# Moving four blocks of a bias table into its main run and three others behind the first scores

## The chip, the cores and the metric

One Trainium2 chip, one of its cores. The time is the device time of one execution in microseconds; for the kernel before it is the median of three runs.

## The reference

Attention with a learned relative bias, then a mixture of experts. Shapes: 8 batches, 8 heads, 576 positions, head size 64, hidden size 32 for the bias.

```python
scores = scale * q @ k.T
psi_rel = log1p(abs(i - j)); psi_i = log1p(max(i, 1))
h = relu((psi_rel / psi_i) * w1 + b1)        # 32 hidden per (i, j)
scores += h @ w2                              # 576 x 576, one per head
attn = softmax(scores); out = attn @ v
# then every token goes through its best of 8 experts, times its gate
```

The bias does not depend on the batch. It is made once, as a table in SBUF, and added to every batch's scores.

## The kernel before

**The table.** The query rows are made in 36 blocks (NBLK). A block covers 16 query rows for all 8 heads: four column groups (cg), each with one hidden tile of 128 partitions (4 rows x 32 hidden) by 576 keys, `relu(window of tg + shift)`, made by `bias_hidden` on ScalarE (L189) for cg 0 and on VectorE (L191) for the others; two matmuls for each (`bias_out`, L199) into PSUM; and one put (`bias_put`): a scaled copy from PSUM on ScalarE (L215) or, for the blocks in PUT_DVE, on VectorE (L213), into one of eight output buffers taken in turn (bias_outs), and from there by DMA into the table. Blocks 0 to 31 (NMAIN) fill `NBm`, the first 512 query rows: block `8c + k` writes rows k, k + 8, ... of the heads of query chunk c, with one DMA (L218) of 288 KB. Blocks 32 to 35 fill `NBr`, the last 64 query rows of two heads at a time, with four DMAs (L223) of 72 KB each. All of these DMAs go through SP's queue, in program order, as do the loads of q, k and v.

**The main run** (`bias_table`) goes through blocks 0 to 31 with three PSUM tiles of two banks. ScalarE's hidden is made one block ahead, and a put is issued one block later (LAG). Hooks run at given blocks: loads and transposes of q and k, steps of the routing's set-up. The table's last blocks are generators (`bias_late`): the first step makes the four hidden, the second the matmuls, into a bank of `eps` and one of `xps`, and the put.

**Attention** (`attention`) goes through pairs of heads n, in five units u each; unit u of a pair makes the scores of 128 queries of both heads (units 0 to 3) or of the last 64 queries of both (unit 4). `ORDER` gives each unit's steps by letters; S is `scores`: twelve matmuls (six in unit 4) into `sps` (L400), and on VectorE the reduction L414 for each head, which adds the table (NBm for units 0 to 3, NBr for unit 4), stores the sum and its minimum. e and f are the exponentials (L429 on ScalarE), t and T the transposes (L444, two units behind), q and k VectorE's transposes of the next pair's q and k. The engines run their instructions in the order written. Unit 3 needs blocks 24 to 31, unit 4 blocks 32 to 35.

In the kernel before the main run ends with the four hidden of block 32, and `LATE` gives the steps of blocks 32 to 35 at the head of units 0 and 1 of the first pair, ahead of their scores; `load_v(0)` follows them at unit 1 (V0). The part of `attention` that places them:

```python
for u, k in self.LATE:
    tail.setdefault((0, u), []).append(lambda k=k: next(self.late[k], None))
tail.setdefault(self.V0, []).append(lambda: self.load_v(0))
```

PSUM: the three tiles of the main run lie where `attn_late` then puts sps0, sps1 and the two eps banks, so the first scores wait for the puts of the last main blocks that used those tiles. SBUF: hidden tiles lie in `eT`, `rT` and, in the main run only, in `Eb`.

Of the kernel before, what the change touches and what calls it, by code (L numbers as in the profile page):

```python
# [40 lines left out]
NMAIN = P // 4  # L41
NBLK = S4 // 4
# [9 lines left out]
def bias_base(blk, cg):  # L52

    if blk < NMAIN:
        return P * (blk // GS) + blk % GS + 4 * GS * cg
    return 4 * P + 2 * (blk - NMAIN) + cg // 2 + 4 * GS * (cg % 2)
# [52 lines left out]
class Attn:  # L109
# [8 lines left out]

    ON_POOL, ON_DVE = (), (1,)


    LAG = 1
    PUT_DVE, ON_ACT2 = (21, 31, 34), ()
    TURN0, SPLIT0, QK1 = (4, 8), (6, 10), (9, 10, 11, 12, 13, 14, 15, 16)
    V0 = (0, 1)
    ROUTE = (6, 7, 8, 15, 16, 18)

    ROUTE_LATE = ((1, 1), (1, 2), (1, 3), (1, 4), (2, 0), (2, 1), (2, 3), (3, 0), (3, 1))  # L130

    LATE_HIDDEN = ((31, 0),)
    LATE = ((0, 1), (0, 0), (0, 2), (0, 1), (0, 3), (1, 2), (1, 3))

    def bias_setup(self):

# [43 lines left out]
    def bias_hidden(self, blk, cg, by):  # L180

        nc = self.nc
        s = bias_base(blk, cg)
        win = self.tg[:, X0 - s : X0 - s + S]
        c = self.shift[:, 4 * blk + cg : 4 * blk + cg + 1]
        h = next(h for h in self.bias_free if blk < NMAIN or not any(h is x for x in self.bias_main))
        self.bias_free = [x for x in self.bias_free if x is not h]
        if by == "act":
            nc.scalar.activation(h, win, AF.Relu, bias=c)  # L189
        else:  # L190
            (nc.gpsimd if by == "pool" else nc.vector).tensor_scalar(h, win, c, 0.0, op0=ALU.add, op1=ALU.max)  # L191
        return h
# [32 lines left out]
    def bias_table(self, hooks):  # L225

        ready = {}
        self.late = [self.bias_late(blk) for blk in range(NMAIN, NBLK)]

        def ahead(blk, cg):  # L230
            if blk < NMAIN and (blk, cg) not in ready:
                by = "pool" if cg == 3 and blk in self.ON_POOL else "act" if cg == 0 and blk not in self.ON_DVE or cg == 1 and blk in self.ON_ACT2 else "dve"
                ready[blk, cg] = self.bias_hidden(blk, cg, by)

        with self.tc.tile_pool(name="bps", bufs=3, space=PSUM) as pp:
            done = []
            for blk in range(NMAIN):
                ps = pp.tile([P, 1024], F32, tag="bps", name=f"bps{blk}")
                if blk + 3 in self.ON_POOL:
                    ahead(blk + 3, 3)  # L240
                for k in range(2):
                    if blk + k not in self.ON_DVE:
                        ahead(blk + k, 0)
                    if blk + k in self.ON_ACT2:
                        ahead(blk + k, 1)
                for cg in range(4):
                    ahead(blk, cg)
                    self.bias_out(cg, ready.pop((blk, cg)), (ps[:, 0:512], ps[:, 512:S]))
                for at, k in self.LATE_HIDDEN:
                    if at == blk:  # L250
                        next(self.late[k])
                if len(done) == self.LAG:
                    self.bias_put(*done.pop(0))
                done.append((blk, [(slice(0, S), ps[:, 0:S])]))
                for f in hooks.get(blk, ()):
                    f()
            for d in done:
                self.bias_put(*d)
# [299 lines left out]
    def attention(self):  # L558
        n_pair = self.n_pair
        tail = self.first_tiles() if self.K else {}  # L560
        for at in self.ROUTE_LATE:
            tail.setdefault(at, []).append(lambda: next(self.route, None))
        for u, k in self.LATE:
            tail.setdefault((0, u), []).append(lambda k=k: next(self.late[k], None))
        tail.setdefault(self.V0, []).append(lambda: self.load_v(0))
        bg = None
        for n in range(n_pair + 1):
            for u in range(5):
                for f in tail.get((n, u), ()):
                    f()  # L570
                if n == 1 and u == 0:
                    bg = self.blanks()
                if u == 4 and n > 0 and n % NP == 0:
                    assert not bg or all(k == len(x) for x, k in bg)
                    bg = self.route_steps(n // NP - 1)
                m, w = (n, u - 2) if u >= 2 else (n - 1, u + 3)
                scored = []
                for op in self.ORDER[u].split():
                    op, self.defer = op[0], int(op[1:] or 0)
                    if op in "aAbc":  # L580
                        self.flush(lambda x: x[0][0] in "er")
                    elif op == "X":
                        self.flush(lambda x: x[0][0] == "a")
                    self.held = [] if self.defer and op in "tTRAc" else None
                    if op in "SefC":
                        if n == n_pair:
                            continue
                        if op == "S":
                            scored = self.scores(n, u)
                        elif op == "C":  # L590
                            self.compact(n, u)
                        else:
                            self.exps(*scored["ef".index(op)])
                    elif op in "tT":
                        if 0 <= m < n_pair:
                            self.etrans(m, w, "tT".index(op))
                    elif op == "x":
                        if n > 0:
                            self.flush(lambda x: x[0][:2] == "av")
                            self.turn_x(n - 1)  # L600
                    elif op in "RaAbc":
                        if n > 0:
                            self.rtrans(n - 1) if op == "R" else self.av(n - 1, *divmod("aAbc".index(op), 2))
                    elif op in "qk01V":
                        if n + 1 < n_pair:
                            if op == "V":
                                self.load_v(n + 1)
                            elif op in "qk":
                                self.turn(n + 1, "qk".index(op))
                            else:  # L610
                                self.split(n + 1, int(op))
                    elif op == "L":
                        if n + 2 < n_pair:
                            self.load_qk(n + 2)
                    elif f := self.route_next(bg, "XB".index(op)):
                        f()
                    fresh, self.held = self.held or [], None
                    for x in self.waiting:
                        x[2] -= 1
                    self.flush(lambda x: x[2] <= 0)  # L620
                    self.waiting += fresh
                if 0 <= m < n_pair:
                    del self.E[m, w]
        self.flush(lambda x: True)
        self.bg = bg
# [867 lines left out]
```

## Time and profile before

| | |
|---|---|
| median of three runs | 1006.18 us (1005.96 to 1006.64) |
| the profiled execution's own time | 1007.5 us |
| its span | 1005.4 us |
| TensorE busy | 972.1 us, 97% |
| VectorE, ScalarE busy | 709.4 us, 712.7 us |
| GpSimd busy | 303.1 us |
| mean granted TensorE clock | 0.995 |

The span is what lies between the first and the last recorded instruction; the execution's own time has what is around it too. In rows, PE is TensorE, PEld its weight loads, DVE VectorE, ACT ScalarE, POOL GpSimd, SP the engine that issues the DMAs; SPq, DVEq and so on are the sequencers. A row of a timeline has a start, a length, the engine, the line in the kernel, the operation, what it writes and reads, its shape, how many are merged, and in brackets how long the engine had been idle and what ended that. A granted clock of 1.00 is TensorE's upper level, 2.4 GHz, and 0.50 its lower, 1.2 GHz.

### The profile page before, as it was taken

How to read it: one execution, taken by the hardware profiler on the slowest of the kernel's cores; microseconds unless marked ns; L12 is line 12 of the kernel's file. 1: busy time of each engine (PE TensorE's matmuls, PEld its weight loads, DVE VectorE, ACT ScalarE, POOL GpSimd, SP SyncE). 2: the span in 40 equal slices, each digit the busy share in tenths (PEclk: the TensorE clock that was granted, in tenths of full speed). 3: DMA queues.
4: the chain of work that ended last, by engine and by line, in shares of the span. 5: the costliest groups of instructions: out<-in, count | busy, mean ns of one | idle time of the engine just before them, and what ended most of it. 6: DMA issues, size and time to landing. Idle time of an engine off the chain costs nothing. (4 is left out here: it accounts for less than half of the span.)

```text
span 1005.4 us, 22478 instructions
## 1 busy us (share of the span) xinstructions
PE 972.1 (97%) x8110; PEld 762.4 (76%) x8110; DVE 709.4 (71%) x1441; ACT 712.7 (71%) x1366; POOL 303.1 (30%) x489
## 2 busy tenths in 40 slices
PE   7969999999999999999999899999999999999997
PEld 4547767767677676776667589889999998989896
DVE  8965768776777777777877677886666656565655
ACT  7977988888888888888888555455555555454554
POOL 1512433625426254262542513511111111111111
PEclk9998999999999999999999999999999999999999
DMA  6977755564655646546469430312117821162610
GB/s 163 194 166 152 196 104 116 109 131 101 128 108 105 134 100 120 119 101 133 94 121 212 128 112 32 96 48 64 43 43 190 271 64 54 61 195 68 186 43 24
DMA packets 327417, 116.34 MB, mean 116 GB/s; under 512 B 283247, under 2 KB 304111, under 8 KB 327299
## 3 DMA queue, kind: packets, MB, share of 16 engines
q1 hardware_dynamic: 321234, 95.80, 43.3%
q0 software_dynamic: 5920, 19.03, 5.4%
q8 instruction: 65, 1.06, 0.5%
q14 instruction: 54, 0.43, 0.2%
q10 hardware_dynamic: 144, 0.00, 0.0%
HBM read 144.34 MB, written 33.34 MB: 177 GB/s over the span
## 5 line engine op out<-in xcount | busy, mean ns | idle before, releaser
L414 DVE CUSTOM_DVE_ANT_0 Eb<-sps,NBm 128x576 f32<-128x576 f32 x256 | 183.6, 754 | 125.0 <-PE sps L400 57.1
L429 ACT ACTIVATE Eb<-Eb,mn 128x576 f32<-128x576 f32 x288 | 221.0, 769 | 13.6 <-DVE mn L414 12.6
L332 ACT ACTIVATE eT<-eps 128x512 f32<-128x512 f32 x256 | 148.9, 595 | 55.7 <-PE eps L444 54.8
L400 PE MATMUL sps<-QK 64*128 64x288 f32 (+1 forms) x1728 | 171.7, 310 | 7.5 <-DVE mn L414 7.0
L400 PEld LDWEIGHTS sps<-QK 64*128 64x128 f32 (+1 forms) x1728 | 134.3, 186 | 48.1 <-DVE mn L414 29.6
L1212 PE MATMUL p<-QK,w1hi 128*128 128x256 f32 x1136 | 161.8, 285 | 2.8 <-DVE QK L1196 2.2
L444 PE MATMUL eps<-idf,Eb 128*128 128x128 f32 x1024 | 149.6, 280 | 3.6 <-DVE eT L334 1.9
L1212 PEld LDWEIGHTS p<-QK,w1hi 128*128 128x128 f32 x1136 | 147.1, 191 | 7.3 <-DVE QK L1196 3.0
L486 PE MATMUL xps<-eT,vraw 128*64 128x288 f32 x1024 | 149.3, 416 | 0.0
L444 PEld LDWEIGHTS eps<-idf,Eb 128*128 128x128 f32 x1024 | 113.3, 141 | 37.5 <-issue 13.6
L1238 POOL DMA_INDIRECT out<-mo,idt x36 | 39.5, 1099 | 308.1 <-ACT mo L1237 252.4
L1214 ACT ACTIVATE hh<-p 128x512 fp32r<-128x512 f32 x72 | 43.1, 598 | 123.0 <-PE p L1212 116.7
L1215 DVE SCALAR_TENSOR_TENSOR hl<-p,hh 128x512 fp32r<-128x512 f32 x72 | 49.7, 691 | 101.6 <-ACT hh L1214 97.8
L1229 PE MATMUL p<-w2hi,hh 128*128 128x512 f32 x288 | 112.3, 390 | 0.0
L1229 PE MATMUL p<-w2hi,hl 128*128 128x512 f32 x288 | 112.3, 390 | 0.0
L434 POOL COPY rem<-Eb 128x128 f32<-128x128 f32 x128 | 37.0, 291 | 244.1 <-ACT Eb L429 238.3
L1174 DVE TENSOR_TENSOR w2lo<-NBm,w2hi 128x1024 fp32r<-128x1024 f32 x72 | 89.5, 1243 | 16.0 <-ACT w2hi L1173 15.7
L486 PEld LDWEIGHTS xps<-eT,vraw 128*64 128x64 f32 x1024 | 62.3, 136 | 39.9 <-issue 12.4
L1212 PE MATMUL p<-QK,w1lo 128*128 128x256 f32 x568 | 91.2, 283 | 0.0
L1174 DVE TENSOR_TENSOR w1lo<-NBm,w1hi 128x1024 fp32r<-128x1024 f32 x72 | 85.0, 1243 | 0.0
L1212 PEld LDWEIGHTS p<-QK,w1lo 128*128 128x128 f32 x568 | 78.3, 192 | 0.0
L1173 ACT CAST w2hi<-NBm 128x1024 fp32r<-128x1024 f32 x72 | 74.9, 1040 | 0.0
(219 smaller groups left out, 1451.0 us busy)
## 6 DMA issues: line engine op xcount, KB each, us to landing
NBm<-moe_w SPq DMA_DIRECT2D x84, 512.0 KB
NBm<-moe_w SPq DMA_DIRECT2D x42, 1024.0 KB
NBr<-xg SPq DMA_DIRECT2D x80, 128.0 KB
kraw<-k SPq DMA_DIRECT2D x128, 72.0 KB
xd<-xt SPq DMA_DIRECT2D x128, 72.0 KB
vraw<-v SPq DMA_DIRECT2D x64, 128.0 KB
NBm<-xTb SPq DMA_DIRECT2D x24, 288.0 KB
NBm<-moe_w SPq DMA_DIRECT2D x3, 2048.0 KB
```

The source lines that it names most:

```text
L332: self.nc.scalar.activation(out, ps, AF.Copy, scale=scale)
L400: nc.tensor.matmul(self.sps[h][:, half, 0:HS], QK[o, q, qs], QK[o, k, HS * half : HS * half + HS], start=i == 0, stop=i == 2, skip_group_c ...
L414: nc.vector.tensor_tensor_reduce(out=e.rearrange("p (t w) -> p t w", t=2), in0=self.sps[h][:, :, 0:HS], in1=nb.rearrange("p (t w) -> p t w ...
L429: self.nc.scalar.activation(e, e, AF.Exp, bias=mn, scale=-1.0, accum_out=sm)
L444: nc.tensor.transpose(ps[:, k, :], e[:, part, P * k : P * k + P], self.idf)
L486: nc.tensor.matmul(ps[out : out + 64, :], lhsT, rhs, tile_position=(row, out), skip_group_check=True, **kw)
L1173: self.nc.scalar.copy(h, w)
L1174: self.nc.vector.tensor_tensor(l, w, h.bitcast(F32), op=ALU.subtract)
L1212: nc.tensor.matmul(ps[:, a, :], w[:, c, fs], x[:, c, :], start=i == 0, stop=i == len(ops) - 1)
L1214: nc.scalar.activation(hh[:, sl, :], ps, AF.Relu)
L1215: nc.vector.scalar_tensor_tensor(hl[:, sl, :], ps, 0.0, hh[:, sl, :].bitcast(F32), op0=ALU.max, op1=ALU.subtract)
L1229: nc.tensor.matmul(ps, h[:, f, sl], m[:, f, :], start=i == 0, stop=i == len(ops) - 1)
```

## The change

The main run now goes by a list, SEQ, of 33 blocks: blocks 0 to 28 in order, with blocks 32, 33, 34 and 35 set in after blocks 7, 11, 15 and 19. Blocks 29, 30 and 31 are made late. Block 29's hidden are made at the end of the main run; its matmuls and put come right behind unit 0's scores, followed by the hidden of blocks 30 and 31; the matmuls and puts of those two come right behind unit 1's scores. Hooks now count positions in SEQ. `load_v(0)` stays at the head of unit 1. PUT_DVE changes from blocks 21, 31, 34 to 21, 29, 31. Two empty options (ON_POOL, ON_ACT2) go.

```diff
--- before.py
+++ after.py
@@ -118,19 +118,19 @@
 
 
 
-    ON_POOL, ON_DVE = (), (1,)
+    ON_DVE = (1,)
 
 
     LAG = 1
-    PUT_DVE, ON_ACT2 = (21, 31, 34), ()
+    PUT_DVE = (21, 29, 31)
     TURN0, SPLIT0, QK1 = (4, 8), (6, 10), (9, 10, 11, 12, 13, 14, 15, 16)
     V0 = (0, 1)
     ROUTE = (6, 7, 8, 15, 16, 18)
 
     ROUTE_LATE = ((1, 1), (1, 2), (1, 3), (1, 4), (2, 0), (2, 1), (2, 3), (3, 0), (3, 1))
 
-    LATE_HIDDEN = ((31, 0),)
-    LATE = ((0, 1), (0, 0), (0, 2), (0, 1), (0, 3), (1, 2), (1, 3))
+    SEQ = (*range(8), 32, *range(8, 12), 33, *range(12, 16), 34, *range(16, 20), 35, *range(20, 29))
+    LATE = ((0, 0), (0, 1), (0, 2), (1, 1), (1, 2))
 
     def bias_setup(self):
 
@@ -183,7 +183,7 @@
         s = bias_base(blk, cg)
         win = self.tg[:, X0 - s : X0 - s + S]
         c = self.shift[:, 4 * blk + cg : 4 * blk + cg + 1]
-        h = next(h for h in self.bias_free if blk < NMAIN or not any(h is x for x in self.bias_main))
+        h = next(h for h in self.bias_free if blk not in self.late_blocks or not any(h is x for x in self.bias_main))
         self.bias_free = [x for x in self.bias_free if x is not h]
         if by == "act":
             nc.scalar.activation(h, win, AF.Relu, bias=c)
@@ -225,34 +225,31 @@
     def bias_table(self, hooks):
 
         ready = {}
-        self.late = [self.bias_late(blk) for blk in range(NMAIN, NBLK)]
+        seq = self.SEQ
+        self.late_blocks = [blk for blk in range(NBLK) if blk not in seq]
+        self.late = [self.bias_late(blk) for blk in self.late_blocks]
 
         def ahead(blk, cg):
-            if blk < NMAIN and (blk, cg) not in ready:
-                by = "pool" if cg == 3 and blk in self.ON_POOL else "act" if cg == 0 and blk not in self.ON_DVE or cg == 1 and blk in self.ON_ACT2 else "dve"
+            if (blk, cg) not in ready:
+                by = "act" if cg == 0 and blk not in self.ON_DVE else "dve"
                 ready[blk, cg] = self.bias_hidden(blk, cg, by)
 
         with self.tc.tile_pool(name="bps", bufs=3, space=PSUM) as pp:
             done = []
-            for blk in range(NMAIN):
+            for at, blk in enumerate(seq):
                 ps = pp.tile([P, 1024], F32, tag="bps", name=f"bps{blk}")
-                if blk + 3 in self.ON_POOL:
-                    ahead(blk + 3, 3)
-                for k in range(2):
-                    if blk + k not in self.ON_DVE:
-                        ahead(blk + k, 0)
-                    if blk + k in self.ON_ACT2:
-                        ahead(blk + k, 1)
+                for b in seq[at : at + 2]:
+                    if b not in self.ON_DVE:
+                        ahead(b, 0)
                 for cg in range(4):
                     ahead(blk, cg)
                     self.bias_out(cg, ready.pop((blk, cg)), (ps[:, 0:512], ps[:, 512:S]))
-                for at, k in self.LATE_HIDDEN:
-                    if at == blk:
-                        next(self.late[k])
+                if at == len(seq) - 1:
+                    next(self.late[0])
                 if len(done) == self.LAG:
                     self.bias_put(*done.pop(0))
                 done.append((blk, [(slice(0, S), ps[:, 0:S])]))
-                for f in hooks.get(blk, ()):
+                for f in hooks.get(at, ()):
                     f()
             for d in done:
                 self.bias_put(*d)
@@ -560,8 +557,6 @@
         tail = self.first_tiles() if self.K else {}
         for at in self.ROUTE_LATE:
             tail.setdefault(at, []).append(lambda: next(self.route, None))
-        for u, k in self.LATE:
-            tail.setdefault((0, u), []).append(lambda k=k: next(self.late[k], None))
         tail.setdefault(self.V0, []).append(lambda: self.load_v(0))
         bg = None
         for n in range(n_pair + 1):
@@ -587,6 +582,8 @@
                             continue
                         if op == "S":
                             scored = self.scores(n, u)
+                            for _, j in (x for x in self.LATE if (n, x[0]) == (0, u)):
+                                next(self.late[j], None)
                         elif op == "C":
                             self.compact(n, u)
                         else:
```

## Rows read from the trace of the kernel before

**Rows 1.** the page, part 1: busy us, share of the span, instructions of each engine

```profile
span 1005.4 us, 22478 instructions
PE 972.1 (97%) x8110; PEld 762.4 (76%) x8110; DVE 709.4 (71%) x1441; ACT 712.7 (71%) x1366; POOL 303.1 (30%) x489
```

**Rows 2.** DVE timeline, 66 to 112 us: start, length, line, operation [idle before <-releaser]

```profile
66.27 0.76 DVE L414 CUSTOM_DVE_ANT_0 Eb<-sps,NBm 128x576 f32<-128x576 f32 x1 [0.44 <-issue]
...
73.68 0.76 DVE L414 CUSTOM_DVE_ANT_0 Eb<-sps,NBr 128x576 f32<-128x576 f32 x1 [4.78 <-DMA vraw<-v]
...
81.34 0.76 DVE L414 CUSTOM_DVE_ANT_0 Eb<-sps,NBm 128x576 f32<-128x576 f32 x1 [3.41 <-PE sps L400]
...
106.26 0.75 DVE L414 CUSTOM_DVE_ANT_0 Eb<-sps,NBr 128x576 f32<-128x576 f32 x1
...
111.22 0.76 DVE L414 CUSTOM_DVE_ANT_0 Eb<-sps,NBm 128x576 f32<-128x576 f32 x1 [1.47 <-PE sps L400]
```

**Rows 3.** timeline of PE (matmuls), 67 to 76 us, same columns

```profile
67.86 1.05 PE L400 MATMUL sps<-QK 128*128 128x288 f32 x6
68.83 1.09 PE L444 MATMUL eps<-idf,Eb 128*128 128x128 f32 x8
74.50 1.81 PE L400 MATMUL sps<-QK 64*128 64x288 f32 x12 [4.58 <-DVE mn L414]
```

**Rows 4.** busy by 2 us stretch: engines, granted clock, DMA share, GB/s

```profile
70.00:72.00 2.00, 0.00 (x0) 0.00 (x0) 0.00 (x0) 0.61 (x2) 0.00 (x0) 1.00 0.40 116
...
74.00:76.00 2.00, 1.50 (x12) 1.46 (x12) 0.45 (x2) 0.87 (x2) 0.00 (x0) 0.50 0.86 143
...
80.00:82.00 2.00, 2.00 (x20) 1.54 (x22) 0.66 (x1) 0.96 (x2) 0.40 (x2) 0.89 0.79 153
```

**Rows 5.** timeline of SP's DMA issues, 44 to 71 us

```profile
44.48 0.55 SPq L218 DMA_DIRECT2D NBm<-xt  x1
...
54.35 0.53 SPq L218 DMA_DIRECT2D NBm<-xt  x1
...
62.83 0.70 SPq L223 DMA_DIRECT2D NBr<-xTb  x1
...
64.14 1.22 SPq L223 DMA_DIRECT2D NBr<-xTb  x2
...
70.59 0.59 SPq L223 DMA_DIRECT2D NBr<-xTb  x1
...
71.22 0.99 SPq L370 DMA_DIRECT2D vraw<-v  x2
```

**Rows 6.** waits of SP's queue, 53 to 80 us: line <- what, us, times, longest

```profile
SPq L223 <- DMA NBm<-xTb: 3.1, 4, 0.9
SPq L223 <- DMA NBm<-xt: 1.0, 2, 0.6
```

**Rows 7.** timeline of DVE, the put of block 31

```profile
53.51 0.82 DVE L213 TENSOR_SCALAR xt<-bps,xrb 128x576 f32<-128x576 f32 x1 [0.58 <-DMA NBm<-xt]
```

**Rows 8.** busy by stretch again: one of 10 us, one of 2 us

```profile
40.00:50.00 10.00, 10.00 (x115) 5.03 (x114) 10.00 (x24) 8.87 (x14) 0.16 (x1) 1.00 1.05 207
...
68.00:70.00 2.00, 1.93 (x15) 1.53 (x14) 0.69 (x1) 2.00 (x6) 1.33 (x2) 1.00 0.38 113
```

**Rows 9.** timeline of DVE: hidden of the last main blocks, then a late put

```profile
50.71 2.22 DVE L191 TENSOR_SCALAR eT<-xTb,xrb 128x576 f32<-128x576 f32 x5
...
59.65 0.74 DVE L213 TENSOR_SCALAR xTb<-eps,xrb 128x512 f32<-128x512 f32 x1
60.31 0.28 DVE L213 TENSOR_SCALAR xTb<-xps,xrb 128x64 f32<-128x64 f32 x1
```

**Rows 10.** timeline of PE: first scores, and the eight matmuls of a late block

```profile
56.85 1.06 PE L400 MATMUL sps<-QK 64*128 64x288 f32 x12
...
57.83 1.09 PE L199 MATMUL eps<-eT,xrb 128*32 128x512 f32 x8
...
59.89 0.22 PE L199 MATMUL xps<-eT,xrb 128*32 128x64 f32 x1
```

## The prediction

> **What bounds the kernel now.** I began with the page: TensorE is busy for 972.1 of 1005.4 us [rows 1], so for nearly the whole span only a place where TensorE waits or runs slowly can give time back. I looked for such places in the stretch that the change touches, the bias table and the first pair (0 to 90 us).
>
> The timeline of VectorE shows one. The first score reduction (L414) of unit 3 of the first pair starts at 66.27. That of unit 4, which alone reads NBr, starts at 73.68 after 4.78 us of idling for a DMA [rows 2]. The row names the load of v, but L414 does not read v; what it reads and what is late is NBr. TensorE has finished everything else by 69.92 (68.83 + 1.09) and idles 4.58 us to 74.50 [rows 3]. It then also runs at half clock: granted 1.00 at 70 to 72 us, 0.50 at 74 to 76, 0.89 at 80 to 82 [rows 4], that is 1.2 GHz until about 80.4 (0.11 of 2 us is 0.44 us at half). What that costs is read from two pairs: from L414 of unit 4 to L414 of the next pair's unit 1 takes 81.34 - 73.68 = 7.66 us there and 111.22 - 106.26 = 4.96 us a pair later [rows 2], so 2.70 us. Stall and clock together are worth about 7.5 us.
>
> Why NBr is late is in SP's issues. Main block 31 was issued at 54.35, but the sixteen NBr DMAs of the four late blocks ran on to 70.59, 0.645 us apart at the end (64.14 to 70.59 is ten steps), and v only follows at 71.22 [rows 5]. Before 64.14 SP's NBr issues waited six times, 4.1 us in all, for older NBm DMAs to land [rows 6]. These waits fit one rule: a DMA is issued when the one eight before it has landed. So block 31's DMA, the eighth before the one at 64.14, took 9.8 us to land. A second sign is the put of block 31, which waits at 53.51 for its buffer, that is for the DMA of block 23 [rows 7], issued at 44.48 [rows 5]: 9.0 us. **The DMA queue is a full eight blocks deep at the end of the table**, one landing each (64.1 - 53.5)/8 = 1.33 us. VectorE is equally full, 10.00 of 10 us, the DMA engines at a share of 1.05 and 207 GB/s; at 68 to 70 us, when only NBr DMAs are out, the share is 0.38 [rows 8].
>
> **Part 1: four blocks of NBr into the main run, three main blocks out.** The work per block is unchanged (four hidden, eight matmuls, one put), and so is the number of blocks. The main run has 33 blocks in place of 32. VectorE pays three hidden for each, five in 2.22 us [rows 9], so 0.44 each and 1.33 a block. In the kernel before, block 32's hidden were already made there, so 33 blocks' hidden end at the same time; block 29's add 1.33, while the put of block 31 on VectorE (0.82 and 0.58 of waiting, [rows 7]) leaves. The first scores need the put of the last block but one, free at about 54.3 (53.5, when its buffer's old DMA has landed, and 0.8), and twelve matmuls of 1.06 us [rows 10]: L414 of unit 0 starts near 55.5.
>
> SP issues four DMAs where it issued one: 3 x 0.645 = 1.9 us more per NBr block, 7.7 us over the run, behind which the later puts queue. It costs TensorE nothing while the eight output buffers cover the delay, and by 47 us, after the last such group, SP is back to one 0.55 us issue per 1.33 us block. If that cover fails, the puts, then PSUM, then TensorE wait.
>
> **Part 2: what is left behind the scores.** VectorE, after unit 0's two reductions (1.4), waits for block 29's matmuls (2.1 from first to last, [rows 10]), puts it (0.74 + 0.28, less overlap 0.95, [rows 9]) and makes six hidden (2.7). Unit 1's L414 then starts near 61.3 (55.5 + 1.4 + about 0.8 of waiting + 0.95 + 2.7); with block 31's put (0.95, ends near 63.7) ahead of the q transpose, unit 3's could start near 67.0, 0.7 later than 66.27. The matmuls of the three blocks lie in TensorE's idle time of this stretch. So the gain of the earlier first scores is spent by unit 3; this is a shift of work between waits, no saving. Behind the put of block 29, which waits for its matmuls on VectorE, stand six hidden and unit 1's reductions; ScalarE's exponentials wait for those.
>
> **Part 3: which wait is last.** NBr lands long before unit 4. But blocks 29 to 31 are rows of NBm that unit 3 reads, one unit sooner, and they are the last in a full queue. SP's order puts the three loads of v, now ahead of unit 1's scores, before blocks 30 and 31. Counting eight back from block 31 (30, three of v, 29, two small ones, the last main block) it cannot be issued before that main block lands, 64.1 + 1.33 = 65.4. Behind it the queue holds block 29, v (as many bytes as a block, costed like one), 30 and 31: 65.4 + 4 x 1.33 = **70.8**. The upper price of an NBr block is a main block's. The lower comes from its own row: share 0.38 x 0.645 = 0.24 us of DMA time per DMA [rows 5, 8], 0.98 per block at a full queue's 1.05 gives 0.93, against 1.33: 0.4 less for each of four, so **69.2**. I take this, the nearest row. At that pace SP's issuing was the limit, the DMA engines were free for most of the time. The Trainium skill, "SBUF — State Buffer", section on the DMA port swizzle, speaks against it: DMA bandwidth depends on how many of SBUF's 16 ports the partitions reach, and by my reading of its map an NBr DMA writes 8 partitions on 4 ports, an NBm DMA 16 on 8. By that page an NBr byte would take twice as long, and the sum would be that of rival 3. The least possible is put (63.7) plus what the last NBr DMA took, 70.59 to 73.68 [rows 2, 5], 3.1: 66.8, which is no wait at all.
>
> From unit 3's L414 to the end of the matmuls ahead of the next pair's first scores there are 69.92 - 66.27 = 3.65 us [rows 2, 3]. The wait stands at the head of VectorE's queue: unit 3's exponentials on ScalarE and unit 4's scores on TensorE wait with it. So the next pair's scores start at 69.2 + 3.65 = 72.85 in place of 74.50: 1.65 gained. TensorE's gap moves forward by a unit: the work ahead of unit 4's scores ends by 67.9 as before, and these start at 69.2 + (67.86 - 66.27) = 70.8 [rows 2, 3]: 2.9 us in place of 4.58. I take it that the clock stays at its upper level then, which gives the 2.70 back. **Sum: -4.35 us.** The profiled execution, to whose rows this belongs, took 1007.5 us around its span of 1005.4; it would take 1003.1. The median of the three runs is 1006.18, which becomes **1001.8 us**. Everything after is bound by TensorE and moves up by the same amount.
>
> **Rivals.**
> 1. Block 31 lands in time (by 67.0). Scores at 70.65: 3.85 + 2.70 = 6.55 gained, **999.6 us**. For it: nothing but the bounds above; against it: queue depth at 54 us.
> 2. The wait only changes its place. The block lands at 70.8, scores start at 74.45, and the gap before unit 4's scores is 4.5 us (72.4 - 67.9), close to the 4.58 after which the clock fell, so it falls again: **1006 us**; with the clock kept, 1003.5. For it: every term of the 70.8 is a measured interval.
> 3. Slower: the NBr DMAs go no faster among the others than alone, 4 x 0.645 = 2.58 us a block against 1.33. Four blocks hold the queue 5.0 us longer, block 31 lands at 75.8, the scores start at 79.45, 4.95 later, with the low clock: **1011 us**. It decides once block 31 lands after 70.9. Against it: at that pace the DMA engines were only 0.38 busy [rows 8], so SP's issuing may have set it. This is the way of the Trainium skill's page "SBUF — State Buffer" above.
> 4. It does not do what it says: unit 4's wait really is for v's queue place [rows 2] or another of SP's, and stays: **1006 us**.
>
> **How the numbers follow.** Forecast 0.38, rival 1 0.20, rival 2 0.22, rival 3 0.10, rival 4 0.10. A measurement of this kernel tells about 0.2% (2 us) from no change. Faster by more than that are the forecast, rival 1 and a little of rival 2 with the clock kept: 0.62; the same: the rest of rival 2, rival 4: 0.28; slower: 0.10. The range leaves out rival 3 and a sliver below rival 1: 999.0 to 1006.6.
>
> **What would show it.** Right: no idle on VectorE before the L414 that reads NBr; a DMA wait of 2 to 3 us before unit 3's two; TensorE's granted clock 1.00 from 60 to 90 us; SP's last bias DMA issued near 66. Wrong: no wait at unit 3 (rival 1), a gap over 4 us with the clock at 0.50 (rival 2), puts of the main run waiting for buffers after 40 us (rival 3), unit 4 still waiting (rival 4).

## The result and the profile after

| | kernel before | changed kernel |
|---|---|---|
| median of five runs each, taken together | 1006.15 us | 1011.61 us |
| profiled execution, and its span | 1007.5, 1005.4 us | 1011.31, 1009.5 us |
| first score reduction, unit 0 of the first pair | 58.30 us | 63.86 us |
| unit 3, where block 31 is needed | 66.27 us | 78.25 us |
| unit 1 of the next pair | 81.34 us | 86.55 us |

The ratio is 1.0058, with a 95% interval from 1.0045 to 1.0072: the changed kernel is **slower by 5.5 us**, where 4.35 us less were forecast. The reductions stand on L411 in it (L414 before), the scores on L397, the put copies and DMAs on L213, L215, L218 and L223 as before.

The page, part 1, lines that answer to [rows 1]:

```profile
span 1009.5 us, 22473 instructions
PE 974.4 (97%) x8110; PEld 761.2 (75%) x8110; DVE 707.2 (70%) x1442; ACT 712.0 (71%) x1364; POOL 308.3 (31%) x489
```

The number of matmuls is the same; TensorE is 2.3 us longer at them and idles more. Where, is seen on VectorE: the reductions that answer to [rows 2], with a put in the main run (timeline of the changed kernel; start, length, line, what it writes and reads, in brackets the idle time before and what ended it):

```profile
46.59 0.82 DVE L213 TENSOR_SCALAR xTb<-bps,xrb 128x576 f32<-128x576 f32 x1 [1.84 <-DMA NBm<-xTb]
...
63.86 0.76 DVE L411 CUSTOM_DVE_ANT_0 Eb<-sps,NBm 128x576 f32<-128x576 f32 x1 [7.37 <-ACT eT L189]
...
69.12 0.75 DVE L411 CUSTOM_DVE_ANT_0 Eb<-sps,NBm 128x576 f32<-128x576 f32 x1
...
78.25 0.76 DVE L411 CUSTOM_DVE_ANT_0 Eb<-sps,NBm 128x576 f32<-128x576 f32 x1 [4.06 <-DMA qraw<-q]
...
81.06 0.76 DVE L411 CUSTOM_DVE_ANT_0 Eb<-sps,NBr 128x576 f32<-128x576 f32 x1 [0.76 <-PE sps L397]
...
86.55 0.76 DVE L411 CUSTOM_DVE_ANT_0 Eb<-sps,NBm 128x576 f32<-128x576 f32 x1 [1.48 <-PE sps L397]
...
111.50 0.75 DVE L411 CUSTOM_DVE_ANT_0 Eb<-sps,NBr 128x576 f32<-128x576 f32 x1
```

The wait of the reduction that reads NBr is gone (0.76 at 81.06, and for TensorE). In its place unit 3 waits 4.06 us, and the first reduction comes 5.56 us later than before. By the third pair the delay is 111.50 - 106.26 = 5.24 us [rows 2], as at the next pair's unit 1 (86.55 - 81.34 = 5.21): all of it arises before 87 us. (The two profiled executions differ by 3.8 us, the medians by 5.5; what else differs later in the run was not followed.)

Why the first reduction is late is seen on ScalarE, which makes most puts (timeline: the put of block 35 and the last two of the main run):

```profile
43.67 0.74 ACT L215 ACTIVATE xt<-bps,xrb 128x576 f32<-128x576 f32 x1 [0.72 <-DMA NBm<-xt]
...
59.97 0.74 ACT L215 ACTIVATE xt<-bps,xrb 128x576 f32<-128x576 f32 x1 [3.39 <-DMA NBr<-xt]
61.13 0.74 ACT L215 ACTIVATE xTb<-bps,xrb 128x576 f32<-128x576 f32 x1 [0.42 <-DMA NBm<-xTb]
```

The put at 59.97 takes the output buffer of block 35, filled eight puts earlier, at 43.67. SP's issues, where the same block is the second L223 group (answers to [rows 5]):

```profile
43.79 2.94 SPq L223 DMA_DIRECT2D NBr<-xTb  x4
46.84 1.87 SPq L218 DMA_DIRECT2D NBm<-xTb  x3
48.80 0.66 SPq L218 DMA_DIRECT2D NBm<-xt  x1
49.56 3.02 SPq L223 DMA_DIRECT2D NBr<-xt  x4
52.68 5.78 SPq L218 DMA_DIRECT2D NBm<-xTb  x6
...
66.66 0.55 SPq L218 DMA_DIRECT2D NBm<-xTb  x1
67.25 1.35 SPq L367 DMA_DIRECT2D vraw<-v  x2
69.48 0.61 SPq L368 DMA_DIRECT2D vrem<-v  x1
70.68 1.93 SPq L218 DMA_DIRECT2D NBm<-xTb  x2
```

Block 35 lies complete at 44.41 (43.67 + 0.74) and is issued from 49.56 to 52.58: SP is five microseconds behind, not back in step as forecast. The last four lines are block 29, the three loads of v, and blocks 30 and 31. TensorE waits at the same place (timeline; answers to [rows 3]):

```profile
61.92 1.81 PE L397 MATMUL sps<-QK 64*128 64x288 f32 x12 [5.42 <-ACT xTb L215]
...
79.07 1.81 PE L397 MATMUL sps<-QK 128*128 128x288 f32 x6 [2.51 <-DVE mn L411]
```

The first row lasts 1.81 us where twelve such matmuls took 1.06 [rows 10], the second 1.81 us where six such took 1.05 [rows 3]: after both gaps TensorE runs at its lower level, 1.2 GHz. The stretches say so (busy of each engine, then granted clock, DMA share, GB/s; answers to [rows 4, 8]):

```profile
30.00:40.00 10.00, 10.00 (x124) 5.47 (x124) 10.00 (x25) 10.00 (x17) 10.00 (x1) 1.00 0.93 157
40.00:50.00 10.00, 9.10 (x100) 4.00 (x94) 8.16 (x20) 6.93 (x11) 6.03 (x1) 1.00 0.76 176
50.00:60.00 10.00, 6.20 (x75) 2.82 (x71) 6.50 (x20) 6.48 (x11) 0.00 (x0) 0.92 1.01 182
...
62.00:64.00 2.00, 2.00 (x16) 1.60 (x20) 0.14 (x1) 1.19 (x2) 0.00 (x0) 0.50 1.06 207
...
80.00:82.00 2.00, 2.00 (x11) 1.99 (x11) 1.07 (x3) 1.39 (x4) 0.29 (x1) 0.50 0.64 125
```

From 40 to 50 us the DMA engines are busier before (1.05, 207 GB/s [rows 8]) than after (0.76, 176). The kernel before has 194 GB/s from 30 to 40 and 218 from 50 to 60:

```profile
30.00:40.00 10.00, 10.00 (x127) 5.53 (x122) 10.00 (x23) 10.00 (x16) 10.00 (x1) 1.00 1.11 194
...
50.00:60.00 10.00, 8.38 (x111) 4.46 (x105) 9.41 (x27) 7.62 (x15) 0.00 (x0) 1.00 1.05 218
```

Over these 30 us, (194 + 207 + 218 - 157 - 176 - 182) x 10 us = 1.04 MB less are moved, 3.5 blocks of 288 KB, or 4.7 us at 1.33 us a block: nearly the delay. What SP waited for from 14 to 54 us, in the kernel before, then in the changed one (us in all, times, longest):

```profile
SPq L218 <- ACT xTb L215: 8.9, 14, 1.3
SPq L218 <- ACT xt L215: 2.6, 3, 1.3
```

```profile
SPq L218 <- ACT xTb L215: 2.5, 4, 0.7
SPq L218 <- ACT xt L215: 0.6, 1, 0.6
```

SP used to wait 11.5 us for ScalarE's puts; now 3.1. The 8.4 us between them is near the 7.7 us of issues that Part 1 counts: most of SP's slack is used up. Whether that, the form of the NBr DMAs or something else makes the table late, the runs have to tell.

### The profile page after: what moved, and what is told of

The parts are those of the page before. It is cut to its first block, busy times and chain, and to the rows that moved or that the text cites. A ratio compares the mean times of both kernels' runs of the same rounds, so it can differ in the third digit from the quotient of the medians.

```text
span 1009.5 us, 22473 instructions
## 1 busy us (share of the span) xinstructions
PE 974.4 (97%) x8110; PEld 761.2 (75%) x8110; DVE 707.2 (70%) x1442; ACT 712.0 (71%) x1364; POOL 308.3 (31%) x489
## 3 DMA queue, kind: packets, MB, share of 16 engines
q8 instruction: 65, 1.06, 0.5%
## 5 line engine op out<-in xcount | busy, mean ns | idle before, releaser
L411 DVE CUSTOM_DVE_ANT_0 Eb<-sps,NBm 128x576 f32<-128x576 f32 x256 | 183.6, 754 | 132.9 <-PE sps L397 51.0
L397 PE MATMUL sps<-QK 64*128 64x288 f32 (+1 forms) x1728 | 172.2, 311 | 10.0 <-ACT xTb L215 5.4
L397 PEld LDWEIGHTS sps<-QK 64*128 64x128 f32 (+1 forms) x1728 | 134.8, 187 | 50.5 <-DVE mn L411 25.3
```

Source lines behind the costliest of these rows:

```text
L397: nc.tensor.matmul(self.sps[h][:, half, 0:HS], QK[o, q, qs], QK[o, k, HS * half : HS * half + HS], start=i == 0, stop=i == 2, skip_group_c ...
L411: nc.vector.tensor_tensor_reduce(out=e.rearrange("p (t w) -> p t w", t=2), in0=self.sps[h][:, :, 0:HS], in1=nb.rearrange("p (t w) -> p t w ...
```

## The experiments

Theory S: SP's issues, four for one, hold the queue up. Theory P: an NBr DMA writes only 8 partitions and is slow in itself, however issued. All times are of one profiled execution unless a median is named; kernels with the same main run start their first reduction up to 0.7 us apart (57.96 and 57.24 below), so differences under that say nothing. Executions of the kernel before, taken beside these runs, lie between 1004.34 and 1008.47 us: a single time in that range is not told from no change, and the argument rests on where the reductions start.

**1. The kernel before with twelve small DMAs more** (`e1_small12`), 640 bytes each, in SP's queue at the puts of four main blocks; nothing narrow is moved.

```diff
...
+        if blk in (8, 13, 18, 23):
+            k = (8, 13, 18, 23).index(blk)
+            for j in range(3):
+                nc.sync.dma_start(self.pad_t[0:32, 3 * k + j : 3 * k + j + 1, :], self.io["c_valid"][0:32, :].rearrange("p (o w) -> p o w", o=1))
...
```

> The kernel before, with three added small DMAs (32 partitions, 20 bytes each, into a tile that nothing reads) on SP's queue behind each put of blocks 8, 13, 18 and 23: as many issues as the change adds to the main run, nearly no bytes. Theory S (the changed kernel is slow because SP has twelve more issues of about 0.65 us in a stretch where it already issues back to back, so puts' DMAs fall behind until the eight output buffers stop the main run): puts wait for buffers from about 43 us on, the first reduction of unit 0 comes 2 to 5 us later than 58.3, and the time is 1008 to 1011 us. Rival P (NBr's transfers themselves hold the DMA engines longer, by their few partitions): no change, first reduction at 58.3, 1006 us.

Measured 1008.12 us (one execution), beside a median of 1006.53 for the kernel before. VectorE's last put of the main run, the first reduction, and the one that reads NBr:

```profile
57.17 0.82 DVE L217 TENSOR_SCALAR xt<-bps,xrb 128x576 f32<-128x576 f32 x1 [3.62 <-DMA NBm<-xt]
...
63.65 0.76 DVE L419 CUSTOM_DVE_ANT_0 Eb<-sps,NBm 128x576 f32<-128x576 f32 x1
...
77.39 0.76 DVE L419 CUSTOM_DVE_ANT_0 Eb<-sps,NBr 128x576 f32<-128x576 f32 x1 [2.87 <-DMA vraw<-v]
```

The issues alone delay the table by 63.65 - 58.30 = 5.35 us. The buffers do not cover them. How, is seen in what SP waits for from 14 to 54 us, and in the stretch from 40 to 50 us:

```profile
SPq L222 <- ACT xTb L219: 4.0, 8, 0.7
SPq L222 <- ACT xt L219: 0.9, 2, 0.7
```

```profile
40.00:50.00 10.00, 9.61 (x109) 4.69 (x101) 10.00 (x23) 7.42 (x12) 0.78 (x1) 1.00 0.80 174
```

SP waits 4.9 us for puts in place of 11.5, and for earlier DMAs to land 1.6 in place of 0.6: its time goes into issuing. The DMA engines meanwhile have less to do, 0.80 and 174 GB/s where the kernel before has 1.05 and 207 [rows 8], nearly as little as in the change (0.76, 176), though nothing here is narrow. Only 1.0 us of that is left at the next pair's unit 1 (82.36 against 81.34): the wait for NBr shrinks by 1.91 us, and this time TensorE's clock stays up behind its gap of 2.67 us:

```profile
78.00:80.00 2.00, 1.79 (x19) 1.63 (x20) 0.71 (x3) 0.97 (x3) 0.00 (x0) 1.00 0.89 147
```

**2. The kernel before with the puts of four main blocks split into four DMAs of 4 partitions each** (`e2_split4`): twelve issues more and narrow ones.

```diff
+            if blk in (8, 13, 18, 23):
+                for g in range(4):
+                    nc.sync.dma_start(self.NBm[32 * g + k : 32 * g + 32 : GS, H * c : H * c + H, :], o[32 * g : 32 * g + 32, :])
...
```

> The kernel before, with the DMA of main blocks 8, 13, 18 and 23 split into four of 72 KB, each from 32 partitions to 4. Nothing else moves. Theory S: like the run with twelve small DMAs within 1 us, 1008 to 1011 us. Rival P: slower than that run by up to 5 us, since each of the sixteen writes few partitions; with P alone and no effect of issues, the small-DMA run is at 1006 and this one at 1008 to 1011.

Measured 1010.06 us. The last put and the first reduction:

```profile
61.98 0.82 DVE L213 TENSOR_SCALAR xt<-bps,xrb 128x576 f32<-128x576 f32 x1 [7.74 <-DMA NBm<-xTb]
...
68.37 0.76 DVE L418 CUSTOM_DVE_ANT_0 Eb<-sps,NBm 128x576 f32<-128x576 f32 x1
```

The first reduction is 4.72 us later still than with as many issues in experiment 1. No more bytes are moved than in the kernel before, so the narrow form costs something of its own, as rival P has it, on top of the issues.

**3. The changed kernel with one DMA for an NBr block** (`e3_one_dma`), 288 KB to 32 partitions: neither issues nor narrowness.

```diff
-            for par in range(2):
-                for a in range(2):
...
+            nc.sync.dma_start(self.NBr[blk - NMAIN : P : 4, :, :], o)
```

> The changed kernel, with each NBr block's put written by one DMA of 288 KB to 32 partitions of NBr, in place of four of 72 KB (the rows of the last 64 queries then lie in the wrong places). Theory S: the main run waits for buffers as little as before the change, the first reduction of unit 0 starts near 55.5 to 57, and what is left is a DMA wait before unit 3 that ends near 69 to 71: 1001 to 1004 us. Rival P would recover too, since 32 partitions are written. If neither holds and the late blocks' order is what costs, the first reduction stays near 56 or 64 and the time stays above 1008 us.

Measured 1005.64 us.

```profile
57.96 0.76 DVE L408 CUSTOM_DVE_ANT_0 Eb<-sps,NBm 128x576 f32<-128x576 f32 x1 [2.31 <-ACT eT L189]
...
72.51 0.76 DVE L408 CUSTOM_DVE_ANT_0 Eb<-sps,NBm 128x576 f32<-128x576 f32 x1 [4.66 <-DMA NBm<-xTb]
```

The whole delay of the first reduction against the kernel before goes, so it lies in the NBr DMAs. The DMA engines are as busy as before from 40 to 50 us:

```profile
40.00:50.00 10.00, 9.65 (x100) 4.19 (x100) 8.58 (x21) 7.80 (x12) 5.60 (x1) 1.00 1.06 206
```

But unit 3 still waits, to 72.51, and the clock falls behind TensorE's gap of 3.11 us there (1.81 us for six matmuls again), so the time only comes back to that of before; the expected 1001 to 1004 us was missed:

```profile
73.33 1.81 PE L394 MATMUL sps<-QK 128*128 128x288 f32 x6 [3.11 <-DVE mn L408]
```

**4. The changed kernel with four DMAs a block, of 32 partitions each** (`e9_wide4`): the issues and bytes of the change, but wide.

```diff
...
+            for j in range(4):
+                nc.sync.dma_start(self.NBr[blk - NMAIN : P : 4, j, :], o[j:P:4, :])
```

> The changed kernel, with an NBr block still written by four DMAs of 72 KB, but each from 32 partitions four apart to 32 partitions four apart, over the whole width of SBUF, in place of 8 partitions of one half (the rows of the last 64 queries then lie in the wrong places). The issues are as many as in the changed kernel. If only the number of issues counts (theory S), the first reduction of unit 0 stays at 62 to 65 and the time at 1010 to 1013 us. If the narrow transfers are a part of it (P), the first reduction comes to 59 to 62 and the time to 1007 to 1010; with P alone 57 to 58 and 1005.6, as with one DMA a block.

Measured 1010.31 us.

```profile
61.54 0.76 DVE L409 CUSTOM_DVE_ANT_0 Eb<-sps,NBm 128x576 f32<-128x576 f32 x1 [4.43 <-ACT eT L189]
```

Between experiment 3 (57.96) and the change (63.86) this splits the 5.9 us: 3.6 for the issues, 2.3 for the narrow form. Both theories hold, S for the larger part. The shares are uncertain by the 0.7 us above.

The Trainium skill, "SBUF — State Buffer", section on the DMA port swizzle, makes DMA bandwidth depend on how many of 16 ports the partitions reach: by my reading 4 for the change's NBr DMAs, 8 for a main block's, 16 here. The runs agree in direction, not in size: by that rule alone, as an estimate, an NBr block would take twice a main block's 1.33 us, 5.3 us more for four and yet more against the wide form used here, where these two runs show 2.3 us. Experiments 1 and 2 show 4.7, with DMAs that write 4 partitions and not 8.

**5. The NBr blocks earlier** (`e4_early`): if SP only needed time to recover, this would give it.

```diff
+    SEQ = (0, 1, 2, 32, 3, 4, 33, 5, 6, 34, 7, 8, 35, *range(9, 29))
```

> The changed kernel, with blocks 32 to 35 at positions 3, 6, 9 and 12 of the main run in place of 8, 13, 18 and 23: most of their sixteen issues fall into a stretch where SP waits for puts for about half of the time. Theory S: fewer waits for buffers, first reduction of unit 0 at 56 to 59, 1002 to 1006 us. Rival P: the same transfers hold the queue as long, first reduction after 60, 1008 us or more.

Measured 1012.77 us, median of four runs, ratio 1.0055 (1.0038 to 1.0071). The expectation fell: puts wait for buffers from 41 us on and the first reduction starts at 63.12, as late as in the change. The last NBr block comes eleven places earlier, and the time in which to recover does nothing. The rows point to the reason: from 10 to 40 us the DMA engines now move 133, 169 and 137 GB/s, where in the kernel before they move 177, 182 and 194, and from 40 to 60 us, behind the groups, 183 and 210 against 207 and 218. What is not moved early is not made up later.

**6. The changed kernel with the next pair's q and k loads on GpSimd's queue** (`e5_qk_gpsimd`): ten issues fewer for SP.

```diff
+        dma = nc.gpsimd if n == 1 else nc.sync
...
```

> The changed kernel, with the ten loads of the second pair's q and k, which stand in the main run, issued on GpSimd's queue in place of SP's. The twelve added NBr issues then nearly have their old room on SP. Theory S (issues on SP): waits for buffers in the main run shrink, first reduction of unit 0 at 56 to 60 in place of 63.9; the wait before unit 3 stays, so 1004 to 1008 us. Rival P (the 72 KB transfers to few partitions hold the DMA engines): first reduction stays after 62, 1009 us or more.

Measured 1015.02 us, worse; the first reduction starts at 65.28, so theory S's 56 to 60 was missed. SP now idles from 35.55 to 38.32 us, and still the put at 60.98 waits 5.41 us for an NBr DMA. But one of GpSimd's issues took 12.26 us and the loads themselves may be slower, so this does not speak clearly for P. It tells nothing on the shares of S and P.

**7. The hidden and puts behind the scores, without Part 1** (`e7_behind_only`): the main run is 0 to 31, the NBr blocks come late as before, but behind the scores.

```diff
+    SEQ = tuple(range(32))
+    LATE = ((0, 0), (0, 1), (0, 2), (1, 1), (1, 3), (1, 2), (1, 3))
+    PUT_DVE = (21, 31, 34)
```

> Part 2 alone: blocks 0 to 31 in the main run as before the change, blocks 32 to 35 late, but their steps behind the scores of units 0 and 1, with v ahead of unit 1. Theory: first reduction near 56 in place of 58.3, but NBr's sixteen issues still come last on SP, now behind v's three: the wait before unit 4 ends at 73 to 76 and the time is 1005 to 1008 us. If the earlier scores are worth something by themselves, under 1004.

Measured 1008.14 us, just above the expected range. The first reduction starts at 55.30, 3.0 earlier than before, and by unit 3 nothing is left (66.86 against 66.27). The NBr DMAs are issued later, to 73.03, and unit 4 waits to 75.47. So Part 2 is a shift between waits, as forecast, and no saving.

**8. Experiment 3 with the loads of v behind blocks 30 and 31** (`e6_one_dma_v_last`):

```diff
-        tail.setdefault(self.V0, []).append(lambda: self.load_v(0))
...
+                            if (n, u) == (0, 1):
+                                self.load_v(0)
```

> The run with one DMA per NBr block, and with the three loads of v moved behind the matmuls and puts of blocks 30 and 31 (the rows of the last 64 queries lie in the wrong places). There the wait before unit 3 ended at 72.5. If v's loads ahead of the two blocks are what delays block 31 (256-byte pieces cost the queue more than a block's bytes), the wait ends 2 to 3 us sooner, near 70, TensorE's gap stays under 4 us, the clock stays at 1.00, and the time is 1000 to 1003 us. If it is the depth of the queue alone, the wait still ends at 72 and the time stays at 1005 to 1006 us.

Measured 1003.50 us.

```profile
69.88 0.76 DVE L408 CUSTOM_DVE_ANT_0 Eb<-sps,NBm 128x576 f32<-128x576 f32 x1 [2.75 <-DMA vraw<-v]
```

The wait ends 2.6 us earlier (1.9 measured from the first reduction, which was 0.7 earlier), so here the v loads ahead seem to have held blocks 30 and 31 up by 1.9 to 2.6 us, more than 1.33; experiments 11 and 12 do not repeat this. Yet the clock falls again, though TensorE's gap ahead of unit 4's scores is only 1.20 us now, with one of 0.86 before that:

```profile
70.70 1.81 PE L394 MATMUL sps<-QK 128*128 128x288 f32 x6 [1.20 <-DVE mn L408]
```

```profile
72.00:74.00 2.00, 2.00 (x11) 1.80 (x9) 0.77 (x2) 1.39 (x4) 0.29 (x1) 0.53 0.52 81
```

**9. The kernel before with half of the NBr DMAs on GpSimd's queue** (`e8_before_nbr_gpsimd`): eight issues on SP instead of sixteen, the same narrow transfers.

```diff
-                    nc.sync.dma_start(self.NBr[r :
+                    (nc.gpsimd if par else nc.sync).dma_start(self.NBr[r :
```

> The kernel before, with eight of the sixteen NBr DMAs (those of the second head of each pair) issued on GpSimd's queue. If SP's issuing (0.645 us each) is what made NBr late, half the issues on a queue with nothing else to do bring NBr's landing from 73.7 to 68.5 to 70.5, TensorE's gap to under 2 us, the clock stays, and the time is 998 to 1002 us. If the transfers to 8 partitions set the pace, or GpSimd's issues are slower than SP's, NBr lands at 72 or later and the time is 1004 us or more.

Measured 1005.13 us, median of ten runs, beside 1006.05 for the kernel before: ratio 0.9993 (0.9984 to 1.0003), no change.

```profile
57.24 9.29 SPq L223 DMA_DIRECT2D NBr<-xTb  x8
```

```profile
72.80 0.76 DVE L414 CUSTOM_DVE_ANT_0 Eb<-sps,NBr 128x576 f32<-128x576 f32 x1 [4.23 <-DMA qraw<-q]
```

SP's last NBr issue ends at 66.53, 4.65 us earlier than before (70.59 + 0.59 [rows 5]), and the reduction starts 0.9 earlier. From 60 to 70 us the DMA engines' share is 0.89, against 0.52 before:

```profile
60.00:70.00 10.00, 7.53 (x66) 5.91 (x62) 6.72 (x17) 9.37 (x23) 6.22 (x10) 1.00 0.89 175
```

So SP's issuing is not the only thing that keeps NBr late. The Trainium skill, "DMA: Bandwidth & Descriptors", section "Issuing engines are not separate DMA queues", says that a second issuing engine saves only the time of issuing; for NBr at the end of the table the trace agrees, with 0.9 us gained of the 4.65 saved in issuing.

**10. The kernel before with fewer and wider NBr DMAs** (`e10_before_gs4`): a block's rows stand four apart, not eight, so that an NBr block goes by two DMAs of 144 KB to 16 partitions each. Main blocks keep one DMA of 16 partitions. No block is moved.

```diff
-GS = 8
-X0 = 4 * P + 8 * GS - 1 - 3 * GS
+GS = 4
+X0 = 4 * P + 64 - 1 - 3 * GS
...
-        return P * (blk // GS) + blk % GS + 4 * GS * cg
-    return 4 * P + 2 * (blk - NMAIN) + cg // 2 + 4 * GS * (cg % 2)
+        return P * (blk // 8) + 64 * (blk % 8 // GS) + blk % GS + 4 * GS * cg
+    return 4 * P + blk - NMAIN + 4 * GS * cg
...
-            c, k = divmod(blk, GS)
-            nc.sync.dma_start(self.NBm[k:P:GS, H * c : H * c + H, :], o)
+            c, k = divmod(blk, 8)
+            k, r = 64 * (k // GS), k % GS
+            nc.sync.dma_start(self.NBm[k + r : k + 64 : GS, H * c : H * c + H, :], o)
...
+                r = 64 * par + blk - NMAIN
+                nc.sync.dma_start(self.NBr[r : 64 * par + 64 : GS, :, :], o[par:P:2, :])
```

> The kernel before, with a block's 16 query rows four apart (one after the other over 64) in place of eight apart, so that an NBr block is written by two DMAs of 144 KB to 16 partitions each in place of four of 72 KB to 8. Order and work are otherwise those of before. Both theories: half the issues and wider transfers bring NBr's landing from 73.7 to 67.5 to 70, TensorE's gap to under 2 us, the clock stays at 1.00: 998 to 1001 us. If what holds NBr back is neither, but the depth of the queue behind the last main blocks, NBr lands at 72 or later, 1004 us or more.

Measured **1002.28 us**, median of nine runs, beside 1006.52 for the kernel before: ratio 0.9954 (0.9941 to 0.9967).

```profile
59.58 8.81 SPq L223 DMA_DIRECT2D NBr<-xTb  x8
...
68.44 1.21 SPq L370 DMA_DIRECT2D vraw<-v  x2
```

```profile
70.90 0.76 DVE L414 CUSTOM_DVE_ANT_0 Eb<-sps,NBr 128x576 f32<-128x576 f32 x1 [0.85 <-DMA vraw<-v]
...
75.87 0.76 DVE L414 CUSTOM_DVE_ANT_0 Eb<-sps,NBm 128x576 f32<-128x576 f32 x1 [1.47 <-PE sps L400]
```

The wait for NBr shrinks from 4.78 us to 0.85, the granted clock is 1.00 in every stretch from 56 to 84 us, and the next pair's unit 1 comes 5.5 us earlier (75.87 against 81.34). The time is a little above the expected 998 to 1001 us. This is about the gain that the change was forecast to bring (4.2 us, forecast 4.35), and it beats both kernels. The main blocks' rows move too, but the gain does not come from them: the first reduction starts at 59.44, 1.1 us later than before.

**11, 12. The change with that same form of the DMAs** (`e11_change_gs4`), and with v behind blocks 30 and 31 as in 8 (`e12_change_gs4_v`). The edits are those of 10 and 8.

> The changed kernel with the same rows four apart: two NBr DMAs a block. The change then adds four issues to the main run in place of twelve, and none is narrow. Expected: first reduction of unit 0 at 57 to 59, the wait before unit 3 until 72 to 73 as with one DMA a block, 1004 to 1007 us. If the main run's loss were due to the order of the blocks and not to their DMAs, the first reduction would stay after 62.

> As the run before it, with v's three loads behind the puts of blocks 30 and 31. Expected: first reduction of unit 0 at 57 to 59, the wait before unit 3 ends near 70, 1002 to 1005 us; slower than the kernel before with rows four apart by 2 to 5 us, if moving blocks into the main run has no gain of its own once NBr's DMAs are cheap.

Measured 1004.84 us (one run) and 1004.72 us (median of ten; ratio 0.9981, 0.9970 to 0.9992). Their first reductions start at 57.64 and 58.27, so the DMAs' form mends the main run; but unit 3 waits to 71.50 and 71.60. Moving v behind thus brings nothing here (0.1 us later; 0.5 earlier when measured from the first reduction), and the expected end near 70 was missed: the 1.9 to 2.6 us of experiments 3 and 8 are not a fixed price of v's loads. In the second, TensorE's gap of 1.89 us there is followed by the lower clock:

```profile
72.42 1.06 PE L397 MATMUL sps<-QK 128*128 128x288 f32 x6 [1.89 <-DVE mn L411]
```

```profile
74.00:76.00 2.00, 2.00 (x10) 1.67 (x11) 0.42 (x2) 1.29 (x4) 0.29 (x1) 0.50 0.57 91
```

So with the DMAs in that form, moving the blocks (and v) costs 2.4 us against experiment 10 (1004.72 and 1002.28, with intervals of the ratios that do not meet).

## Why the prediction was wrong

**The step that failed** is Part 1's "It costs TensorE nothing while the eight output buffers cover the delay, and by 47 us, after the last such group, SP is back". The term was priced at nothing. The first reduction came 63.86 - 55.5 = 8.4 us after the forecast and 5.56 after the kernel before; 5.9 of the 8.4 go away with the NBr DMAs' form (experiment 3), the other 2.5 are below. SP issued the last group at 49.56 to 52.58, the put eight later waited 3.39 us for it, and TensorE idled 5.42 us and came back at 1.2 GHz. The price of the issues was near (the last two groups of four took 2.94 and 3.02 us on SP, where 4 x 0.645 = 2.58 were counted); their cover was not there. The prediction's own reading said so: it found the queue "a full eight blocks deep at the end of the table" and a put already waiting for its buffer [rows 7]. Buffers that are full can cover nothing. It had also read the DMA engines at a share of 1.05 from 40 to 50 us [rows 8], and did not ask what they do while SP issues four pieces for one. SP had slack, 11.5 us of waiting for puts; the engines it feeds had none. With the extra issues they move 174 to 176 GB/s there in place of 207 (the change, experiment 1), without them 206 (experiment 3), and what is not moved then comes late.

**The price per NBr block** was taken between 0.93 and 1.33 us, from the DMA share while SP paced alone [rows 8]. Experiments 1, 2 and 4 show that both terms count, issuing and width, and 9 that issuing is not the only one. The reason that set rival 3 aside, DMA engines only 0.38 busy, was half true: SP did pace them then, but with half of the issues elsewhere the share went to 0.89 and NBr landed hardly earlier.

**Part 1's 55.5** was 2.5 us too early even where the NBr DMAs cost no more than main ones (57.96 in experiment 3): it counted only part of a block's way through the buffers. With the main run at 32 blocks and nothing else ahead of the scores the first reduction did start at 55.30 (experiment 7). That a 33rd block in a run paced by one landing each 1.33 us is the reason is argued, not shown.

**Part 2** was right: a shift between waits (experiment 7). **Unit 4's wait** does go, as forecast, so rival 4 falls.

**Part 3** was right in kind, wrong in size. The last wait is unit 3's, for block 31. With the main run mended it ends at 72.51 (experiment 3) or 71.50 (11) and not at 69.2 or 70.8. What v's loads cost, "costed like" a block at 1.33, stays open: 1.9 to 2.6 us in one pair of runs (3 and 8), at most 0.5 in the other (11 and 12). In the change it ended at 78.25, where the delay of the main run comes on top.

**The clock** was taken to stay up behind a gap of 2.9 us. In the traces, one execution each, it fell behind 2.51 us in the change, 3.11 in experiment 3, 1.89 in 12, and in 8 behind gaps of 0.86 and 1.20; it stayed up behind 2.67 us in experiment 1. The length of one gap does not decide it, and the forecast had no ground for the 2.70 us that it gave back. Executions of one kernel differ too: the ten of experiment 12 have mean granted clocks from 0.994 to 0.999, and the fastest, 1003.0 us, is the one at 0.999.

**Rivals.** Rival 3's 1011 us was hit, in part by luck. Its sign in the profile, puts that wait for buffers after 40 us, was there, and its 5.0 us for four blocks is near the 5.9 that their form cost. Its place was not there: it let the queue be late only behind the main run (block 31 at 75.8), while the larger part was lost ahead of the first scores. Rival 2 is what remains once the main run is mended (experiment 3: a gap of 3.11 us where it has 4.5, the low clock, 1005.64 us against its 1006).

**Open:** the exact split of issuing and width (single executions), why the width costs 2.3 us in one pair of runs (8 partitions a DMA against 32) and 4.7 in the other (4 against DMAs of almost no bytes), whether a narrow DMA is slow for the ports that it reaches or for how many DMA engines take part in it, what v's loads cost, and what decides whether the clock falls behind a gap.

## What to carry to other kernels

Before issues are added to a queue, look whether the DMA engines that it feeds and the buffers behind it are full already: if they are, time that the issuing engine spends waiting is not slack, and further issues are paid almost in full (5.35 us for twelve, experiment 1). Where a late table holds a stage up, first mend the form of its transfers (fewer DMAs, more partitions in each), and move work only if that is not enough; here the form alone gave 4.2 us (experiment 10), and moving the blocks on top took 2.4 back (12). Price a moved wait by the clock too, and keep both levels in the range.

## What was not expected of the hardware

Twelve DMAs of 640 bytes in SP's queue delayed the table by 5.35 us (experiment 1), 0.45 us each, near the 0.55 us that a main block's issue takes [rows 5]. The same 288 KB in four DMAs cost 3.6 us more over four blocks than in one, even at 32 partitions each (experiments 3 and 4). And TensorE's clock fell from 2.4 to 1.2 GHz at two gaps of about a microsecond (experiment 8), while it kept its level across one of 2.67 us (experiment 1).
